# Loading batch 0's first four tiles as one four-token interleave, with the causal tokens computed by products over 11 rows of each tile

## The chip, the cores and the metric

One core of a Trainium2 chip. The metric is the device time of one execution in microseconds, in which a profiled execution's span (first to last instruction) lies about 1.5 us below its time. Engines: PE is TensorE (matrix products), DVE VectorE, ACT ScalarE, POOL GpSimd, SP SyncE.

## The reference, cut to what matters

Four batches, eight heads, 768 tokens, head size 40; an mLSTM cell, then a maxout MLP on 3072 tokens.

```python
for t in range(S):
    m_new = np.maximum(f_gate[:, :, t] + m, i_gate[:, :, t])
    f_stab = np.exp(f_gate[:, :, t] + m - m_new); i_stab = np.exp(i_gate[:, :, t] - m_new)
    C = f_stab * C + i_stab * (v_t outer k_t);  n = f_stab * n + i_stab * k_t
    y[:, :, t] = sigmoid(o_gate_t) * (C q_t) / max(|n q_t|, 1)
h1 = x @ w1; h2 = x @ w2
out = np.maximum(h1, h2) @ w_out        # x is y as [3072, 320]; w1, w2: 320 x 1024
```

The kernel uses that, with these gates, only the first 42 tokens of a sequence contribute to C and n. It checks this on the chip; if it does not hold, PE and the other engines branch into a general block after the fast part. These inputs never enter that block. Tokens below 42 are causal (a mask over keys); all later ones use the finished state. The maxout is rewritten as relu(x(w1 - w2)) w_out + x (w2 w_out), so a unit of token pairs needs an "up" part (products with wd = w1 - w2 into pu), a relu (gt), and a "down" part (products with wo and with Wc_t = w2 w_out into po).

## The kernel before, where the change and the argument touch it

```python
UNITS = [[0, 1], [2], [3, 4], [5, 6], [7, 8], [9, 10], [11]]   # pairs of token tiles
SEG = ((0, 1), (1, 4), (4, 6))        # batch 0 is loaded as tile 0, tiles 1-3, tiles 4-5
...
def f_h(n, pool=None, eng=V, dup=V):  # output of the cell for token tile n
    first = c == 0                    # tile 0: 128 tokens in order, masked scores
    ...
    if n % 2:                         # copy the last 64 columns for the other lanes
        cp(dup)(out=y[:, DM:DM + 64], in_=y[:, 2 * DM:2 * DM + 64])
    cp(eng)(out=nqb[:, n, :], in_=ph[:, :, D])
...
# start-up, in program order (cut)
A.copy(out=kb[:, 1:B]..., in_=warm...);  A.copy(out=vw[:, 1:B]..., in_=warm...)
f_k(0, pp_o); idle(2)                 # idle(n): n filler products, meant to keep PE's clock up
...
f_q(1, A, 2); sig_first(0, V); f_h(0, pp_o)
f_q(3, V, 1); sigm(0, 1, 2); sigm(0, 2, 4); idle(3)
f_h(1, pp_o, V, A); f_h(2, None); f_h(3, pp_o, V, A)     # the copies of y on ACT
...
# end
with tc.If(general > 0), ExitStack() as gctx:    # general block, not entered here
    ...
```

## Time and profile before

| | before |
|---|---|
| time, median of 3 | 96.98 us (96.98 to 97.0) |
| the profiled execution | 97.5 us, span 96.0, clock 1.0 |
| PE, DVE, ACT, POOL busy | 89.0, 54.8, 42.5, 28.0 us |
| first MLP product, first output product | 13.61, 24.79 us |
| last copy of an output out of PSUM (where PE's products land) | 93.09 to 93.38 us |

PE is busy nearly throughout. What matters is when its dense part (from the first output product on) begins. The profiled execution was 0.5 us slower than the median.

### The profile page before, as it was taken

Reading aid. Unit: us, or ns where it says so; the run is one execution under the profiler, and the core shown is the slowest. Engines: PE = TensorE matmul, PEld = TensorE weight load, DVE = VectorE, ACT = ScalarE, POOL = GpSimd, SP = SyncE. Lnnn points to the kernel's source line nnn. Section 1 sums busy time; section 2 is a strip of 40 time slices with the busy share of each in tenths; the row PEclk is TensorE's granted clock in tenths of the full one; section 3 lists DMA queues with packets and bytes.
Section 4 is the critical chain, followed back from the end, with each engine's and each line's share of the span. In section 5 each row is a group of like instructions: output and inputs, shape, how many; then the busy total and the mean of one; then the engine's idle time right before and its main releaser. Section 6 shows DMA issues by size and latency. Waiting matters only on the chain.

```text
span 96.0 us, 2281 instructions
## 1 busy us (share of the span) xinstructions
PE 89.0 (93%) x875; PEld 65.1 (68%) x875; DVE 54.8 (57%) x164; ACT 42.5 (44%) x63; POOL 28.0 (29%) x67
## 2 busy tenths in 40 slices
PE   3999979899889999999999999999999999999970
PEld 1347546766479788788787866768676777786660
DVE  4978926952368999597852535976054352240340
ACT  0886693861523771192809067080623408404000
POOL 5054596755655442623154000044000000000000
DMA  0999999997999999996999899697712030311052
GB/s 13 171 268 332 386 387 373 354 241 127 309 292 243 215 215 360 306 116 113 295 279 104 121 296 300 165 108 85 205 68 72 0 137 10 138 70 68 7 205 68
DMA packets 34045, 18.29 MB, mean 191 GB/s; under 512 B 23152, under 2 KB 31792, under 8 KB 34032
## 3 DMA queue, kind: packets, MB, share of 16 engines
q1 hardware_dynamic: 32594, 17.90, 75.7%
q10 hardware_dynamic: 1438, 0.23, 1.5%
q8 instruction: 7, 0.11, 0.5%
q14 instruction: 6, 0.05, 0.2%
HBM read 12.42 MB, written 3.93 MB: 170 GB/s over the span
## 4 chain that ended last, share of the span: by engine, by line
PE 56%; DMA 23%; SPq 11%; DVE 4%; ACT 2%; issue 1%; DVEq 0%
PE po L510 21%; DMA ost<-in_o_gate_dram 17%; PE pu L464 14%; PE po L506 6%; DMA w<-in_moe_w_dram 6%; PE pu L472 5%; SPq L118 3%; PE ph L357 3%; SPq L380 3%; DVE y L367 2%; PE pq L298 2%; SPq L104 2%; PE po L494 2%; ACT ost L267 2%; PE py L389 1%
## 5 line engine op out<-in xcount | busy, mean ns | idle before, releaser
L481 ACT ACTIVATE gt<-pu 128x1024 bf16<-128x1024 f32 x18 | 17.6, 1021 | 27.3 <-PE pu L472 27.3
L510 PE MATMUL po<-wo,gt 128*128 128x320 bf16 x160 | 26.9, 299 | 0.0
L464 PE MATMUL pu<-xT,wd 128*128 128x256 bf16 (+1 forms) x224 | 24.9, 257 | 1.0 <-DVE xT L390 0.7
L518 DVE COPY o_sb<-po 128x320 f32<-128x320 f32 (+2 forms) x23 | 10.9, 474 | 20.4 <-PE po L510 20.3
L464 PEld LDWEIGHTS <-wd 128*128 128x128 bf16 x224 | 19.0, 98 | 3.7 <-POOL wdx L408 0.8
L510 PEld LDWEIGHTS <-gt 128*128 128x128 bf16 x160 | 15.0, 98 | 5.2
L367 DVE SCALAR_TENSOR_TENSOR y<-ost,ph 128x320 bf16<-128x320 f32 x20 | 9.6, 481 | 3.1 <-PE ph L357 2.0
L267 ACT ACTIVATE ost<-ost 128x320 f32<-128x320 f32 (+2 forms) x14 | 8.7, 657 | 4.7 <-DMA ost<-in_o_gate_dram 4.7
L506 PE MATMUL po<-Wc_t,xT 128*128 128x320 bf16 (+2 forms) x50 | 10.7, 296 | 0.0
L222 PE MATMUL pd<-warm,ident_b 128*128 128x512 bf16 x25 | 8.9, 479 | 1.7 <-POOL ident_b masks.py:199 1.7
L257 POOL CAST qb<-qst 128x240 bf16<-128x240 f32 (+1 forms) x12 | 5.8, 485 | 11.7 <-DMA qst<-in_q_dram 9.9
L472 PE MATMUL pu<-xT,wd 64*128 64x256 bf16 (+1 forms) x112 | 7.7, 256 | 0.0
L357 PE MATMUL ph<-cq,qT 120*128 120x123 bf16 (+1 forms) x60 | 6.0, 213 | 0.7 <-DVE nqb L371 0.4
L481 ACT ACTIVATE gs<-pu 128x512 bf16<-128x512 f32 x8 | 4.3, 591 | 5.0 <-PE pu L472 5.0
L357 PEld LDWEIGHTS <-qT 120*128 120x128 bf16 (+1 forms) x60 | 4.4, 98 | 2.7 <-DMA qT<-qb 0.7
L402 POOL TENSOR_TENSOR wd<-w 128x512 bf16<-128x512 f32 x4 | 5.1, 1270 | 2.9 <-DMA w<-in_moe_w_dram 2.7
L506 PEld LDWEIGHTS <-xT 128*128 128x128 bf16 x50 | 3.9, 97 | 2.8 <-issue 1.8
L510 PE MATMUL po<-wo,gs 128*128 128x320 bf16 (+2 forms) x40 | 5.8, 272 | 0.0
L472 PEld LDWEIGHTS <-wd 64*128 64x128 bf16 x112 | 4.0, 94 | 2.4 <-issue 1.3
L538 POOL TENSOR_TENSOR a<-i_sb,F 32x640 f32<-32x640 f32 x1 | 1.5, 1532 | 12.4 <-DVE F L536 12.4
L222 PEld LDWEIGHTS <-ident_b 128*128 128x128 bf16 x25 | 2.5, 116 | 3.7 <-POOL ident_b masks.py:199 1.7
L494 PE MATMUL po<-Wc_t,xT 64*128 64x320 bf16 (+2 forms) x25 | 3.6, 292 | 0.4 <-ACT Wc_t L442 0.4
(126 smaller groups left out, 112.2 us busy)
## 6 DMA issues: line engine op xcount, KB each, us to landing
qst<-in_q_dram SPq DMA_DIRECT2D x3, 800.0 KB, 5.8
ost<-in_o_gate_dram SPq DMA_DIRECT2D x3, 800.0 KB
out_dram<-o_sb SPq DMA_DIRECT2D x7, 320.0 KB
w<-in_moe_w_dram SPq DMA_DIRECT2D x8, 256.0 KB, 5.6
out_dram<-o_sb SPq DMA_DIRECT2D x9, 160.0 KB, 3.7
wo_st<-in_moe_w_out_dram SPq DMA_DIRECT2D x2, 640.0 KB
qst<-in_q_dram SPq DMA_DIRECT2D x4, 160.0 KB
wx<-in_moe_w_dram SPq DMA_DIRECT2D x2, 256.0 KB
```

Of the source, the lines that this page charges most:

```text
L222: nc.tensor.matmul(pd[:, 0, :], ident_b, warm, start=True, stop=True)
L257: cp(eng)(out=qp[b % 2][:, c0:c1, 0:2, 0:HS3 * D].rearrange("p c s (h d) -> p c s h d", d=D), in_=qst[b][:, 0:6, c0:c1, :].rearrange("p (s ...
L267: A.activation(out=s, in_=s, func=AF.Tanh, scale=0.5)
L357: nc.tensor.matmul(ph[:, vcols(s), :].rearrange("p a b -> p (a b)"), lhsT, rhs[:, vcols(s), :].rearrange("p a b -> p (a b)"), start=True, ...
L367: V.scalar_tensor_tensor(out=yo, in0=ost[b][:, :, c, :], scalar=1.0, in1=ph[:, :, 0:D], op0=OP.add, op1=OP.mult)
L464: nc.tensor.matmul(pus[i][:, j, :], wd[:, c, f * 128:(f + 1) * 128], x[:, :, GA[i][c], :], start=(c == 0 and (j % 2 == 0 if np_ == 2 else ...
L472: nc.tensor.matmul(pus[i][:, j, :], wd2[r, f * 128:(f + 1) * 128], x[r, :, 2, :], start=False, stop=(j == 3 if np_ == 1 else j % 2 == 1))
L481: A.activation(out=o, in_=pus[i], func=AF.Relu)
L494: nc.tensor.matmul(po, xT[u][r, s // 2, 2, :], Wc_t[r, 2, w], start=True, stop=False)
L506: nc.tensor.matmul(po, x[:, s // 2, GA[s % 2][cc], :], Wc_t[:, cc, w], start=False, stop=False)
L510: nc.tensor.matmul(po, gt[:, f, s % 2, s // 2 * L:(s // 2 + 1) * L], wo[:, f, w], start=False, stop=(f == NFF - 1))
L518: cp(eng)(out=o_sb[:, s % 2 if two else 0, :], in_=po)
```

## The change

The intent: q and o_gate of batch 0's first four tiles in one load of 640-byte runs instead of runs of 160 and 480, so that the first loads and the weights behind them land earlier; the first 42 tokens then lie in rows 0 to 10 of each of four tiles, where short products overwrite the state's result. Single-pair units do both halves of their up part in one piece. Two transposes move from the DMA queue to PE, and the slots between the units' pieces are reordered.

```diff
-    SEG = ((0, 1), (1, 4), (4, 6))
+    SEG = ((0, 4), (4, 6))
+    TC = 11
...
+    G.tensor_copy(out=F[:, L:L + NS * KP]..., in_=ident_f[:, 0:H9].unsqueeze(2).to_broadcast([BH, H9, T0]))
     G.memset(sel, 0.0)
...
-    def f_h(n, pool=None, eng=V, dup=V):
+    def h_parts(n, pool=None, eng=V, dup=V):
...
+        if n < 4:
+            yield
+            for s in range(NS):
+                nc.tensor.matmul(ph[0:TC, vcols(s), :]..., Pm[0][m, s, c, :], vb[0][m, vcols(s), :]..., ...)
...
+    def up_one(u):                       # a single-pair unit: all 8 blocks, then all 64-row products
...
-    A.copy(out=vw[:, 1:B]..., in_=warm...)
+    G.memset(fold, 0.0) ; G.affine_select(fold...)      (moved up)
+    G.memset(vw[:, 1:B], 0.0)
...
     f_k(0, pp_o)
     idle(2)
     f_v(0, pp_o)
...
-    f_h(1, pp_o, V, A)
-    f_h(2, None)
-    f_h(3, pp_o, V, A)
+    parts = [h_parts(n, (pp_o, pp_f, pp_f, pp_o)[n]) for n in range(4)]
+    for g in parts:
+        next(g)
...
-    G.tensor_copy(out=wo[:, 4:8], in_=wo_st[:, 4:8])
-    sigm(0, 4, 6)                        (moved behind the close of Wc_t)
+    G.tensor_copy(out=wo[:, 4:6], in_=wo_st[:, 4:6])
+    A.copy(out=wo[:, 6:8], in_=wo_st[:, 6:8])
...  (the slot plan: X10, X16 become y10, y16, and most others move)
```

## The prediction

> **What bounds the kernel now.** I read the engine shares first, then engine busy time by stage, then the chain that ended last, then the timeline of the first 25 us. The shares give PE 89.0 of 96.0 us, but 8.9 us of that are filler products with the tile pd (25 of them), all in the start-up. So I cut the span into three stages, by two events that the timeline shows: the first MLP product at 13.6 and the first output product at 24.8. The columns are length of the stage, then busy time and count of each engine.
>
> ```profile
> core 0: us, PE busy (x) PEld busy (x) DVE busy (x) ACT busy (x) POOL busy (x), PEclk, DMA share, GB/s
> 1.60:13.50 11.90, 11.06 (x71) 5.68 (x71) 9.68 (x40) 8.65 (x16) 5.95 (x20) 1.00 1.04 285
> 13.50:24.80 11.30, 10.42 (x102) 7.63 (x102) 6.30 (x10) 6.31 (x11) 7.76 (x8) 1.00 1.02 277
> 24.80:92.70 67.90, 67.21 (x701) 51.58 (x701) 37.96 (x110) 27.54 (x38) 13.60 (x36) 1.00 0.73 169
> ```
>
> The reader is to see that from 24.8 to 92.7 PE idles for 0.69 us in all: that part gets shorter only by taking PE work away. PE's dense part starts at 24.8, and what matters is what sets that date. A piece of the chain from the dense part, start and length in us:
>
> ```profile
> 72.84 0.54 PE pu L472 x8
> 73.38 0.14 PE po L494 x2
> 73.52 0.38 PE po L506 x2
> 73.90 1.09 PE po L510 x8
> ```
>
> Eight products of 320 columns take 1.09 us, 136 ns each. The 64-row products (L472, L494) run in pairs and cost more than their columns[...]. So a passage into 64-row products and out again costs about 0.22 us.
>
> The chain in the start-up:
>
> ```profile
> 7.56 5.76 DMA w<-in_moe_w_dram
> 13.34 10.33 DMA ost<-in_o_gate_dram
> ...
> 23.69 0.74 ACT ost L267
> 24.43 0.32 ACT Wc_t L442
> ...
> 24.79 0.31 PE po L494 x2
> ```
>
> The gate load of batch 0's last two tiles lands at 23.7. ACT, in order, does its tanh (L267) before it closes Wc_t, for which PE waits 0.41 us. The timeline shows the two other walls:
>
> ```profile
> 7.75 0.72 POOL L262 CAST qb<-qst 128x640 bf16<-128x640 f32 x1 [0.80 <-DMA qst<-in_q_dram]
> ...
> 12.97 0.49 DVE L390 COPY xT<-py 128x640 bf16<-128x640 bf16 x1 [0.86 <-PE py L389]
> ...
> 13.61 1.03 PE L464 MATMUL pu<-xT,wd 128*128 128x256 bf16 x8 [0.68 <-DVE xT L390]
> ...
> 20.95 1.25 POOL L644 CAST wo<-wo_st 128x1280 bf16<-128x1280 f32 x1 [0.98 <-DMA wo_st<-in_moe_w_out_dram]
> ```
>
> q of tiles 1 to 3 lands at 7.75; from it hangs the chain cast, transposes, h, y, transposes, xT (13.46), first MLP product (13.61). The second half of wo lands at 20.9, its cast ends at 22.2, and 12 products with wo (12 x 136 = 1.63) plus six transposes (0.34) must follow: 24.2. Both loads are bound by the DMA engines, busy throughout; how fast they move depends on the run length (last two columns: share and GB/s):
>
> ```profile
> 4.00:5.50 1.50, 1.50 (x7) 0.82 (x6) 1.39 (x12) 1.27 (x3) 0.00 (x0) 1.00 1.27 211
> 6.00:8.00 2.00, 2.00 (x14) 1.02 (x13) 1.20 (x5) 1.46 (x3) 1.12 (x5) 1.00 1.21 297
> 10.00:12.00 2.00, 1.79 (x19) 1.16 (x19) 2.00 (x9) 1.26 (x4) 1.25 (x1) 1.00 1.06 389
> ```
>
> In the first stretch the runs are mostly 160 bytes (k, v, one tile of q and o_gate), in the second 480 (three tiles interleaved), in the third 2048 (weights).
>
> [...]
>
> **The change, part by part.** (a) Loads. Per run and engine the times are 16 x 160 / 211 = 12.1 ns, 16 x 480 / 297 = 25.9 and 16 x 2048 / 389 = 84. A line between the last two gives about 32 ns for 640 bytes, or 320 GB/s. Before, k, v and the first tile of q and o_gate (0.43 MB) take 2.05 us and the other three tiles (0.98 MB) 3.3: together 5.35. After, k and v take 0.5 and 1.31 MB at 320 GB/s 4.1: together 4.6. So all weights land about 0.8 us earlier. q of all four tiles no longer has any o_gate beside it: 0.14 MB are through by about 3.3 us, 0.66 MB at 320 GB/s take 2.05, and 0.9 us more pass until the release (as before, where the bytes ahead of q's end were through at about 6.8): 6.3 instead of 7.75.
>
> (b) The y chain. It gets longer: tile 0 no longer goes ahead alone. From q at 6.3: two half casts on ACT and POOL at once (0.72) to 7.0; PE is busy with the v and c products until about 7.4, as DVE's row reaches only then; transposes (0.35), ACT copy of qT (0.80) to 8.6, DVE's beside it to 8.7; the mask product (0.35), 3 score products, P0 at about 9.4; 12 main and 12 short products (some 55 ns each, as five PE transposes in the chain take 0.28; 1.25 together) 8.9 to 10.2; four y of DVE with copies of 0.18 and 0.16 between, from 9.8 to 12.0; the second pair's transposes 12.2 to 12.5, its xT at 13.1. But the first MLP products are now done pair by pair (8 of 128 columns, 0.45), so PE starts at 12.5 instead of 13.6, and the fold products (0.43) fill the wait for the second pair. Gain 1.1.
>
> (c) From first MLP product to dense part, 11.2 us before. Pure PE work there is the first unit's up part 4.58, 20 transposes 1.1, fold 0.43, 24 products with wo 3.27, six transposes 0.34: 9.7. The remaining 1.5 is mostly waiting: the 0.41 for Wc_t goes (tanh moved behind it), and the first relu now starts after half the last products, so its buffer frees 0.4 earlier. PE then reaches the products with the second half of wo at about 20.8. wo: landing 20.9 - 0.8 = 20.1, and the cast is halved between POOL and ACT (0.65 instead of 1.25): also about 20.8. From there 1.63, a close of 0.49 and a little: dense part at 23.0 to 23.3 instead of 24.8. Gain of (a) to (c) together: 1.5 to 1.8; I take 1.6.
>
> (d) Dense part. Two DMA transposes (pairs 5 and 8 of y) become PE transposes: 10 x 55 ns = +0.55 us of PE. Units of a single pair in one piece: one passage of 64-row products less per unit (about 0.12 for the first, 0.22 for the last): -0.35. All other PE counts are the same (the order of both kernels lists 160 + 40 output products, 48 transposes of q, and so on, in each). Of the 0.69 us of PE idle, the worst piece, at 60 us, waited on DVE behind an o_gate load and a DMA transpose; two DMA transposes less (1.2 to 3 us of queue each) should save about 0.3. Sum about -0.1. ACT's 8 relu of 0.59 become 4 of 1.02: 0.6 us less, off the path.
>
> Sum: -1.6 - 0.1 = -1.7, so 95.3 us.
>
> **The rivals.** First: the y chain eats the load's gain. The trace for it: DVE and ACT are the tight engines there (9.7 and 8.7 of 11.9 us), every y costs 0.48 on DVE, and all four now come after the mask. Against: MLP work begins with pair 0. If so, PE starts at 13.6, and only (c)'s 0.6 to 0.8 remains: 96.1. Second: wo keeps the date. If weights land no earlier (from the ninth load on, each issue waits for the landing of the load eight places before it, so the program may hold them back), the cast at 20.9 + 0.65 leaves a start at 24.0, 0.8 gained: 96.1. Third: the dense part pays. DVE is busy 4.5 and 4.7 of 5 us between 30 and 40, and two copies of 0.49 come on top; with work 1.6 us earlier, loads of batches 1 to 3 have less time (DMA share near 1 until 60 us). New PE waits of 0.5 to 1 us would give 95.8 to 96.3. A fourth goes the other way: the later waits were all DMA, and PE loses none any more: 94.8.
>
> **Range and chances.** The start-up gain lies between 0.8 and 2.1, the dense part between -0.6 and +0.6. That is 94.4 to 96.3. The 2% line is at 95.04, only 0.26 below my number, so faster by over 2% gets 0.36. Slower by over 2% needs +1.9 us, for which I see nothing: 0.02.
>
> **What would show it.** q's first cast at about 6.3; first MLP product near 12.5; first wo-half casts near 20.1; first product into po near 23.2; from there to the last product 67.8 us with PE idle under 0.6. If the y chain starts PE at 13.5 or later, step (b) is wrong; if wo's last cast begins after 20.6, step (a); if the dense part is above 68.3, step (d). Fewer than 17 fillers matter only if PE's products there get slower than 55 ns per 128 columns.

The sum came to -1.6 (start-up) and -0.1 (dense part), -1.7 in all, so 95.3 us. The 0.22 can be had from the trace of before: sixteen products of 256 columns take 1.75 us there (from 71.09), 109 ns each, so four would take 0.44 where the four 64-row pairs took 0.54; two products of 320 columns at 136 ns would take 0.27 where the two after them took 0.38. That makes about 0.21.

## The result, and the profile after

The change measured 99.44 us median (98.49 to 101.45, four runs) against 96.98. The fast runs give a ratio of 1.0169 (95% interval 1.0149 to 1.0189): slower by 1.7%, where I had predicted 95.3. The profiled execution was a slow one (101.45 us, span 100.0). Its page, the granted clock in tenths in 40 slices of 2.5 us:

```profile
PEclk9996559999999999999999999999999999999999
```

Then engine busy time by stage, with the same three stages as in the prediction, the cuts laid near this kernel's own events (the last one at its first output product, 27.72):

```profile
1.60:14.60 13.00, 11.30 (x66) 7.24 (x68) 9.42 (x33) 5.76 (x8) 9.11 (x22) 0.76 0.98 323
...
27.80:95.40 67.60, 67.46 (x714) 52.22 (x714) 39.97 (x113) 26.10 (x33) 11.36 (x29) 1.00 0.55 143
```

The clock (column 7) was 0.76 on average in the first stage, and the dense part began 2.9 us later than before. The dense part itself is no worse: 67.6 us, with PE idle 0.14 us in it. A slow execution does not explain the fast ones, so the fast start-up must be read elsewhere. The experiment a5_shortgen below executes exactly the same instructions as the change and its profile is fast; it stands for the change in the fast state up to the last output. In it the first MLP product comes at 13.93 and the first output product at 24.86: no earlier than before (13.61 and 24.79).

```profile
1.60:13.90 12.30, 11.17 (x81) 6.38 (x82) 10.89 (x40) 6.89 (x11) 8.56 (x22) 1.00 0.98 319
13.90:24.80 10.90, 10.52 (x117) 8.09 (x117) 7.00 (x15) 6.93 (x12) 6.84 (x9) 1.00 1.00 277
24.80:92.64 67.84, 67.67 (x717) 52.25 (x714) 40.49 (x113) 26.33 (x33) 12.88 (x33) 1.00 0.59 158
```

DVE was busy 10.89 us in the first stage against 9.68 before. Its timeline there, a5_shortgen, with start, length and the idle time before:

```profile
4.51 0.94 DVE L246 CAST kb<-kst 42x320 bf16<-42x320 f32 x1
...
6.60 0.80 DVE L249 TENSOR_TENSOR vw<-vst,gT 42x328 bf16<-42x328 f32 x1
```

and that of POOL in the same execution:

```profile
4.26 1.02 POOL L643 MEMSET vw<- 128x1107 bf16 x1
6.34 0.72 POOL L268 CAST qb<-qst 128x640 bf16<-128x640 f32 x1 [1.06 <-DMA qst<-in_q_dram]
```

The same two instructions of DVE before:

```profile
4.24 0.31 DVE L240 CAST kb<-kst 42x320 bf16<-42x320 f32 x1
...
6.94 0.49 DVE L243 TENSOR_TENSOR vw<-vst,gT 42x328 bf16<-42x328 f32 x1
```

The cast of 42x320 took 0.94 us instead of 0.31 and ended 0.17 us after POOL's memset. The product of 42x328 took 0.80 instead of 0.49, beside POOL's cast of q, which ended 0.34 us before it. That DVE stood still in them until POOL was done is my reading of these times; a2_dupact, a3_poollate and c3_dupv below put it to the test. What in the chip makes it wait, the traces do not show.

The second finding is at the other end. From the page's list of queues, and from the waits of SP, the change:

```profile
q8 instruction: 8, 0.13, 0.6%
```

```profile
SPq L953 <- DMA out_dram<-o_sb: 2.0, 1, 2.0
```

and before:

```profile
q8 instruction: 7, 0.11, 0.5%
```

```profile
SPq L882 <- DMA out_dram<-o_sb: 0.4, 1, 0.4
```

q8 moves blocks of 16,384 bytes, and how many goes with the length of PE's program (eight in the change, seven in a5_shortgen, which has 76 PE instructions less and is otherwise the same), so I take them for PE's instructions. The change has one more than before, and it starts at 96.4 us, 1 us after the end of PE's last product; before, the last one starts at 90.3 us, ahead of the last outputs. SP's last wait, for the last output, grew from 0.4 to 2.0 us. From the end of the last copy out of PSUM to the end of the span it is 2.6 us before and 4.2 after.

So there were two theories for the fast executions, and one for the slow ones: (1) DVE waits for POOL in the start-up (0.63 and 0.31 us in the two lines above) and gives back what the earlier load gains; (2) a late instruction fetch (96.37 to 97.30 us) delays the last output; (3) the wait that (1) puts on PE (1.3 us in the change's slow profile) lets its clock fall in some executions.

### The profile page after: what moved, and what is told of

It reads as the page before. It is cut to its first block, busy times and chain, and to the rows that moved or that the text cites. A ratio compares the mean times of both kernels' runs of the same rounds, so it can differ in the third digit from the quotient of the medians.

```text
span 100.0 us, 2338 instructions
## 1 busy us (share of the span) xinstructions
PE 91.2 (91%) x910; PEld 68.8 (69%) x911; DVE 59.4 (59%) x170; ACT 39.9 (40%) x54; POOL 29.1 (29%) x68
## 3 DMA queue, kind: packets, MB, share of 16 engines
HBM read 12.42 MB, written 3.93 MB: 164 GB/s over the span
## 4 chain that ended last, share of the span: by engine, by line
PE 76%; DMA 11%; DVE 6%; issue 1%; SPq 1%
PE po L575 26%; PE pu L505 17%; PE po L571 7%; DMA ost<-in_o_gate_dram 6%; PE pu L513 5%; DMA w<-in_moe_w_dram 5%; PE ph L375 3%; PE pwc L465 3%; PE pu L479 3%; PE py L415 2%; PE po L559 2%; PE pq L304 2%; DVE y L391 2%; DVE gt L519 1%; PE pu L486 1%
## 5 line engine op out<-in xcount | busy, mean ns | idle before, releaser
L505 PE MATMUL pu<-xT,wd 128*128 128x256 bf16 (+1 forms) x176 | 20.9, 263 | 0.3 <-DVE gt L519 0.3
L505 PEld LDWEIGHTS <-wd 128*128 128x128 bf16 x176 | 15.5, 98 | 3.1 <-issue 0.6
L273 ACT ACTIVATE ost<-ost 128x640 f32<-128x640 f32 (+2 forms) x13 | 8.3, 693 | 0.0
L227 PE MATMUL pd<-warm,ident_b 128*128 128x512 bf16 x16 | 6.5, 528 | 1.9 <-POOL ident_b masks.py:199 1.7
L513 PE MATMUL pu<-xT,wd 64*128 64x256 bf16 x80 | 6.1, 272 | 0.0
L489 ACT ACTIVATE gs<-pu 128x1024 bf16<-128x1024 f32 x4 | 3.9, 1021 | 4.9 <-PE pu L486 4.9
L375 PEld LDWEIGHTS <-qT 120*128 120x128 bf16 (+1 forms) x63 | 4.9, 108 | 1.1 <-DVE nqb L397 0.2
L416 DVE COPY xT<-py 128x640 bf16<-128x640 bf16 x7 | 3.4, 491 | 2.4 <-PE py L415 1.9
L227 PEld LDWEIGHTS <-ident_b 128*128 128x128 bf16 x17 | 1.9, 126 | 4.1 <-issue 2.4
L305 DVE COPY qT<-pq 128x768 bf16<-128x768 bf16 x7 | 3.8, 553 | 1.3 <-PE pq L304 1.3
```

The costliest lines, as they stand in the source:

```text
L227: nc.tensor.matmul(pd[:, 0, :], ident_b, warm, start=True, stop=True)
L273: A.activation(out=s, in_=s, func=AF.Tanh, scale=0.5)
L375: nc.tensor.matmul(ph[:, vcols(s), :].rearrange("p a b -> p (a b)"), lhsT, rhs[:, vcols(s), :].rearrange("p a b -> p (a b)"), start=True, ...
L505: nc.tensor.matmul(pus[i][:, j, p0 * L:p1 * L], wd[:, c, f * 128:(f + 1) * 128], x[:, p0:p1, GA[i][c], :], start=start and j % 2 == 0 and ...
L513: nc.tensor.matmul(pus[i][:, j, :], wd2[r, f * 128:(f + 1) * 128], x[r, :, 2, :], start=False, stop=stop and j % 2 == 1)
```

## The experiments

Twelve kernels compared with before in five rounds. They ran in four jobs, each on one chip and all four chips different; before measured 97.21, 97.23, 97.19 and 97.12 us in them. All results were correct.

### a0_again: the change once more

No edit.

> The changed kernel once more, unchanged, for a profile that fell into full clock and for how often the low clock comes. Clock theory (the tensor engine's idle 1.3 us at 6.3 to 7.6 us and thin work after it let the clock fall to 0.5 for some 7 us in some runs): times scatter from 98.5 to 101.5 as before, the granted clock falls as the time rises, and in a run at clock 1.0 the first output product starts near 26.5 instead of 27.8. Rival (the scatter is the chip's, not this kernel's): the kernel before, in the same rounds, scatters too.

Measured: 99.99 us median (98.06 to 101.43, six runs), ratio of the fast ones 1.0149 [1.0110, 1.0188]. Profile slow again, at half clock for the same 6.83 us as above. The two states of the change are reproducible, and before, in the same rounds, had no slow execution.

### a1_fill: four more filler products ahead of the v product

```diff
     f_k(0, pp_o)
-    idle(2)
+    idle(6)
     f_v(0, pp_o)
```

> Four more filler products ahead of the v product, so that the tensor engine is not idle there. Clock theory: every run at clock 1.0, no run above 99, median near 98.5, that is about 1 us below the changed kernel's median; nothing gained over its fast runs. Rival (the start-up is set by the vector engine's and GpSimd's chain, the clock is a bystander): same scatter or a shift of all runs, the fast ones included.

Measured: 98.99 us (98.44 to 99.17, five runs), ratio 1.0176 [1.0151, 1.0202]; no slow execution (though two of 99.17, where I had expected none above 99), clock 0.997 in the profile. In the slow profile of the change, PE waited before the v product:

```profile
PE pv L337 <- DVE vw L249: 1.3, 1, 1.3
```

and these are its stretches around that wait (busy times as above, the seventh column the clock):

```profile
5.00:6.50 1.50, 1.17 (x8) 0.64 (x8) 1.50 (x11) 1.11 (x3) 0.27 (x1) 1.00 1.13 356
6.50:8.00 1.50, 0.30 (x1) 0.13 (x1) 1.41 (x4) 0.71 (x1) 1.20 (x4) 1.00 1.13 364
8.00:10.00 2.00, 1.90 (x17) 1.70 (x16) 1.25 (x4) 0.87 (x2) 0.09 (x1) 0.57 1.06 387
10.00:15.00 5.00, 4.79 (x35) 3.86 (x36) 2.42 (x6) 1.19 (x2) 4.77 (x4) 0.50 1.05 383
```

PE had 0.30 us of work between 6.5 and 8.0; from 8.27 it ran at half clock for 6.83 us, in which it was busy 6.61 us. The clock records of that trace come in stretches of 3.41, 6.83 and 85.33 us, which are one, two and 25 times 3.41; I call a stretch of 3.41 us, counted from where the records begin, a window. In both slow profiles the first window, at full clock, began at 4.9 us and held the whole wait: PE was busy for 52% (the change) and 60% (a0_again) of it, and the next two windows were at half clock. In the two fast profiles of kernels with the wait, a5_shortgen and a2_dupact, the first window at full clock began only at 6.5 and 6.1 us, the wait was 0.6 and 0.5 us, and PE was busy for 77 and 80% of the window. With the wait bridged (a1_fill, from 4.9 us) it was 81%. So in these five profiles the state goes with where the windows fall on the wait; what decides it in general they do not show. Slow were 11 of the 23 executions of kernels with the wait (the change, a0_again, a2_dupact, a5_shortgen), and none of 44 of those with it bridged or removed (a1_fill, a3_poollate, a4_all, a6_allshort and the four of c1_loops to c4_best). So (3) is right for the slow executions that were profiled, but it is about the slow ones alone: the fast time stayed where it was, with the first MLP product at 13.95 and the dense part at 24.88. This is the prediction's own last sentence come true: the change has fewer fillers, and they mattered.

### a2_dupact: the copies of y on ACT

```diff
-    parts = [h_parts(n, (pp_o, pp_f, pp_f, pp_o)[n]) for n in range(4)]
+    parts = [h_parts(n, (pp_o, pp_f, pp_f, pp_o)[n], V, A) for n in range(4)]
```

> The two 64-column copies of y in the start-up go back to ScalarE, as in the kernel before. In the changed kernel they took 0.82 and 0.47 us on VectorE, where the same copy takes 0.18 elsewhere, while GpSimd ran weight subtractions. [...]first MLP product 0.6 to 0.9 us earlier and the fast time 0.5 to 0.9 lower. Rival (the copies stretch, but the weight loads or ScalarE set the pace): under 0.2 us.

The words cut here, and in a3_poollate and c3_dupv, named a cause inside the chip, which no run shows; what was tested is whether DVE's instructions take longer beside POOL's.

Measured: 98.53 us (98.08 to 101.28, two of six slow), ratio 1.0117 [1.0095, 1.0140]: 0.3 us below the change's in a0_again, which the two intervals do not separate, and less than the 0.5 to 0.9 expected. The first MLP product came at 13.48, the dense part at 24.41, 0.45 us earlier than in a5_shortgen. But 0.31 of that is not the edit's: in this execution DVE's v product began at 6.61 us, 0.01 ahead of POOL's cast of q; it took 0.49 us, and POOL's cast 1.06 instead of 0.72. In a5_shortgen the cast began first, and the v product took 0.80. The copies themselves, from the first y to the first MLP product, were 0.14 us (2.67 against 2.81): a small part of the loss as the change is timed.

### a3_poollate: POOL's copy and memset behind its cast of q

```diff
-    G.tensor_copy(out=F[:, L:L + NS * KP]..., in_=ident_f[:, 0:H9]...)     (ahead of all other POOL work)
-    G.memset(vw[:, 1:B], 0.0)                                               (behind the fold's mask)
...
     pad_q(1)
+    G.tensor_copy(out=F[:, L:L + NS * KP]..., in_=ident_f[:, 0:H9]...)
+    G.memset(vw[:, 1:B], 0.0)
```

> GpSimd's selector copy into F and its zeroing of vw, both new in the start-up before 5.3 us, are moved behind the q cast, into GpSimd's idle time at 7.7 to 9.9 us. [...]VectorE's cast of kb comes back from 0.94 to about 0.31 us and its v product from 0.99 to about 0.49, the v product on the tensor engine starts about 1 us earlier (6.6 instead of 7.64), the idle gap shrinks to 0.3, the clock stays at 1.0 in most runs, and the fast time falls by 0.5 to 1.0. Rival (other things set the start of the v product): the casts stay long, less than 0.2 us.

Measured: 99.15 us (98.95 to 99.46, four runs, none slow), ratio 1.0203 [1.0181, 1.0225]: 0.5 us slower than the change's fast runs, where 0.5 to 1.0 less was expected. The trace says where the gain went. The cast of k was back at 0.30 us, the v product 1.2 us earlier at 6.3, the first y at 10.6 instead of 11.1. Then the first copy of y took 1.16 us, from 11.48, and the first MLP product came at 14.1. The earlier chain had moved that copy onto a POOL instruction, as in c3_dupv below: POOL's subtraction wdx ran from 11.33 to 12.60, and the copy ended at 12.64. It also speaks for (3) following from (1): with the wait gone, no slow execution of four, and none in the later kernels that have this edit.

### a4_all: the three edits of a1, a2 and a3 together

> The changed kernel with three edits at once: four more filler products after the score products, the copies of y for the second pair's other lanes taken from VectorE to ScalarE, the selector copy and the memset of GpSimd put behind its pad copy. Theory (the start-up is lost to VectorE waiting for GpSimd, the clock fall to the idle PE, and both gains were given back one step later when only one was mended): no slow execution, kb cast about 0.30 us, v product at about 6.3 us, copies of y short, first MLP product at 12.5 to 12.9, dense part from 23.3 to 23.9, last output copy ending about 1 us earlier than in a1_fill (92.2), and the tail of 3.9 to 4.4 us unchanged, so 97.3 to 98.0 us. Rival (the weights or the wo casts set the dense start whatever y does): first MLP product early but dense start still 24.5 or later, time 98.3 to 99.

Measured: 98.26 us (97.92 to 98.89, six runs, all fast), ratio 1.0111 [1.0075, 1.0146]. A miss: I had expected 97.3 to 98.0. First MLP product at 13.24, dense part at 24.17, where I had expected 12.5 to 12.9 and 23.3 to 23.9. The v vector was ready at 6.46, but PE was in the six fillers until 7.08: here the fillers held back by 0.62 us the work that they were to bridge to, as it came early. The tail was 4.2 us, as in the change, and as expected.

### a5_shortgen: the change with fewer PE instructions in the block that is never entered

```diff
-                for j in range(c + 1):
-                    nc.tensor.matmul(pH[:, c, :], Pa[:, j, c * L:(c + 1) * L], v1[:, j, :], ...)
+                nc.tensor.matmul(pH[:, c, :], Pa[:, c, c * L:(c + 1) * L], v1[:, c, :], start=True, stop=True)
...  (one of three products into pu, one of eight into po, likewise; wrong on purpose if it were entered)
```

> The changed kernel with PE instructions cut out of the general block, which these inputs never enter (its result would be wrong if it were entered; on purpose): 1894 PE program rows instead of 1970, before has 1909; nothing that is executed differs. Theory (an eighth 16 KB instruction fetch behind PE's last product shares a DMA engine with the last output and delays it): seven fetches instead of eight, none behind the last product, wait for the last output 0.3 to 0.6 us instead of 1.6 to 2.2, from last output copy to end about 2.6 us; fast executions 1.3 to 1.8 us below the changed kernel's, so 96.6 to 97.4; slow executions stay. Rival (the longer tail comes from the single-piece last units or the output transfers themselves): eight or seven fetches, but the tail stays at 3.9 or more and the time at 98.5.

Measured: two fast runs, 97.35 and 97.59, and four slow ones, 100.05 to 101.06; too few fast ones for an interval. Their mean, 97.47, is 1.2 us below that of the change's fast runs (98.65 in a0_again, on another chip with the same time of before). Its queue and SP's wait:

```profile
q8 instruction: 7, 0.11, 0.5%
```

```profile
SPq L947 <- DMA out_dram<-o_sb: 0.7, 1, 0.7
```

Nothing that is executed differs, only the program's length, and what the trace shows of that is that the late fetch is gone. Two of the four slow executions (100.08 and 101.06) are listed at clock 1.0 and left no trace; before's trace has no clock record at all and is listed at 1.0 too, so a 1.0 need not mean full clock, and what slowed these two stays open.

### a6_allshort: a4_all with the same cut

> a4_all with the same cut in the general block: 1902 PE rows. If the start-up theory and the fetch theory hold and add: 95.5 to 96.4 us, every execution fast, faster than the kernel before by 0.8 to 1.5 per cent. If only the fetch theory holds: 96.7 to 97.3. If neither: 98 to 99.

Measured: 97.14 us (96.39 to 97.32, six runs, all fast), ratio 0.9969 [0.9932, 1.0006]; 1.12 us below a4_all on the same chip, the same fetch effect a second time. In its profile the first fillers followed each other at 0.43 us instead of 0.21 (its clock records begin, at full clock, only at 7.28), and the v product started only at 7.89, so the dense part began at 24.83: less than I had expected of the start-up, for the reason named under a4_all.

### b1_longgen: the kernel before with a longer block that is never entered

```diff
-            for c in range(NT):
-                for j in range(c + 1):
+            for _ in range(3):
+                for c in range(NT):
+                    for j in range(c + 1):
...
```

> The kernel before with the head loop of the general block, never entered, written out three times: 1993 PE rows instead of 1909; nothing that is executed differs. Fetch theory: an eighth instruction fetch behind PE's last product, wait for the last output 1.6 to 2.2 us instead of 0.4, time 98.2 to 98.9 (slower by 1.3 to 1.9 per cent). Rival (rows that aren't executed cost nothing): 97.0 to 97.3, the same.

Measured: 98.15 us (97.88 to 98.44, six runs), ratio 1.0090 [1.0059, 1.0121]. The old kernel, none of whose executed instructions was touched, becomes 0.9% slower (I had expected 1.3 to 1.9):

```profile
q8 instruction: 8, 0.13, 0.6%
```

```profile
SPq L883 <- DMA out_dram<-o_sb: 1.4, 1, 1.4
```

This settles (2). How it comes about, as far as the traces tell: PE's program comes in seven to eight blocks of 16,384 bytes for some 2000 instructions, fetched while PE works (before: seven, starting from 18.6 to 90.3 us, 9 to 16 apart). A longer branch shows too, but it costs nothing here: PE's branch over the block takes 0.68 us in b1_longgen, 0.37 in the change and 0.24 before, while PE's next instruction waits for a semaphore until 0.77 to 0.81 us after the branch's start in all three, and the eighth fetch starts only 1.4 to 1.7 us after it. What was late were packets of the last outputs: in the trace of the change the eighth block is fetched from 96.37 to 97.30, and 16 packets of the last two outputs, eight of 128 from each, go one after another from 97.28 to 98.12, when all others had landed by 96.93. That is a sixteenth of each output, what one of the 16 DMA engines carries if they share evenly (the trace does not name the engine of a packet), and it is 1.2 us late; in b1_longgen the same share is 0.95 us late. So the fetch of a further block, some 1.5 us after the jump, seems to stand in one DMA engine's way when the last outputs have to leave; that it is one engine, and that the jump causes the fetch, are inferred from the packets' number and the order in time.

### c1_loops, c2_x, c3_dupv and c1_forced

c1_loops has a3's and a2's edits, the change's own two fillers, and a general block that is complete but has loops in place of unrolled products (1902 PE instructions by my count). c2_x takes the two transposes back to the DMA queue; c3_dupv puts the copies of y back on DVE; c1_forced enters the block.

```diff
 c1_loops, general block
-            for f in range(NFF):
+            with tc.For_i(0, NFF, 1) as f:
...  (also for the heads' sum; its transposes by DMA)
 c2_x, against c1_loops
-C3.1.3|h17|            ... x20|y16||||        (and y10, likewise)
+C3.1.3|h17|X16         ... x20|||||
 c3_dupv, against c1_loops
-    parts = [h_parts(n, (pp_o, pp_f, pp_f, pp_o)[n], V, A) for n in range(4)]
+    parts = [h_parts(n, (pp_o, pp_f, pp_f, pp_o)[n]) for n in range(4)]
 c1_forced, against c1_loops
-    with tc.If(general > 0), ...
+    with tc.If(general > -1), ...
```

> The changed kernel with GpSimd's selector copy and memset behind its pad copy and the copies of y on ScalarE, fillers as in the change (in a4_all and a6_allshort the four extra fillers themselves held the v product back by 0.6 and 1.4 us), and a general block that is complete but has its products in loops: 1902 PE rows. Theory: v product at about 6.4 us, y from about 10.0, first MLP product at 12.5 to 12.8, dense part from 23.4 to 23.8, dense part 67.7 to last output copy, tail 2.6: 95.2 to 96.2 us, 1 to 2 per cent faster than before. Rival (without the extra fillers the clock falls in some executions): a spread up to 99 or more, slow executions. Rival (the gain is again eaten by another wait): 96.5 to 97.3.

Measured: 98.23 us (97.92 to 98.79, six runs, all fast), ratio 1.0131 [1.0105, 1.0158]. A miss, and not of the start-up: first MLP product 13.03 (I had expected 12.5 to 12.8), dense part 23.96 (23.4 to 23.8), last copy out of PSUM ending at 91.99, 0.6, 0.8 and 1.4 us earlier than in before's profile (0.3, 0.9 and 0.9 against that of b1_longgen). The rest went in a tail of 4.3 us. With the loops the program had again an eighth block, fetched at 92.2, although by my count it is no longer than a6_allshort. That count leaves out what the loops add: PE's instruction file is 130,048 bytes long for c1_loops and 126,848 for a6_allshort, which is 2032 and 1982 instructions of 64 bytes (the change and a5_shortgen differ by 4,864 bytes for 76 instructions). Of the eleven kernels whose list of queues was read, those with 1973 to 2013 fetched seven blocks and those with 2032 to 2063 eight (before 1979, the change 2049).

> c1_loops with the copies of y back on VectorE, as the change has them. [...]the first copy waits for GpSimd's weight subtraction to end and takes about 1.1 us instead of 0.24 on ScalarE, the next y products come later, first MLP product 0.9 to 1.4 us later, time 0.6 to 1.3 us above c1_loops. Rival (a3_poollate lost its time to something else): within 0.3 us of c1_loops.

Measured: 98.81 us (98.54 to 99.33, five runs), ratio 1.0168 [1.0144, 1.0192]; 0.6 us above c1_loops by the medians, 0.4 by the ratios. Timeline of DVE and of POOL:

```profile
11.26 1.16 DVE L392 COPY y<-y 128x64 bf16<-128x64 bf16 x1
```

```profile
11.12 1.26 POOL L432 TENSOR_TENSOR wdx<-wx 128x512 bf16<-128x512 f32 x1
```

A copy of 64 columns began 0.14 us after POOL's subtraction, and ended at 12.42, 0.04 after it. On ACT the same copy takes 0.24 (c4_best). The first MLP product and the dense part came 0.92 us later than in c1_loops. Theory (1) holds for this part as well.

> c1_loops with the transposes of the sixth and ninth pair back on the DMA queue, as the kernel before has them, in earlier slots: ten PE transposes less. If the dense part is bound by PE's own work alone: 0.4 to 0.6 us less than c1_loops (each five transposes took about 0.27 us of PE time). Rival (the transposed pairs arrive late or delay the loads): the same or slower, with waits of PE for xT.

Measured: 97.20 us (96.84 to 97.62, six runs), ratio 0.9994 [0.9974, 1.0014]; 1.0 us below c1_loops. The number is better than I had expected, but not for the reason: from the first output product to the last copy it took 67.90 us, c1_loops 67.74. PE had 0.37 us less work between 24 and 91 and waited 0.37 more. The gain came from the tail: with 20 PE instructions less there was no eighth 16 KB block. Yet 3.9 us passed from the last copy to the end. Its queues and SP's wait:

```profile
q8 instruction: 7, 0.11, 0.5%
q14 instruction: 8, 0.07, 0.3%
```

```profile
SPq L955 <- DMA out_dram<-o_sb: 1.1, 1, 1.1
```

q14 moves blocks of 8,192 bytes, of which before, the change, a1_fill and a4_all to b1_longgen have six; here two more ran from 93.3 to 94.4 us, and the eight packets of the last output that are one DMA engine's even share landed by 94.1, 0.6 us after all others. My loops had lengthened the programs of the other engines (c1_loops has 205, 79, 126 and 81 instructions on DVE, ACT, POOL and SP by my count, c4_best below 192, 67, 113 and 71 and again six blocks), so I take these blocks for theirs.

> c1_loops with the general block entered on purpose after the fast path, to see whether its rewritten form computes the reference: correct, and far slower (hundreds of us to some ms).

Measured: correct, 2601 us. The rewritten block is right.

### c4_best and c4_forced: a general block without loops

The start-up of c1_loops, one of the two transposes (X16) on the DMA queue, and a complete general block with transposes by DMA and products of 512 columns instead of 128: 1906 PE instructions by my count, and fewer on the other engines than c1_loops has.

```diff
-            for f in range(NFF):
-                pu = pp_u.tile([128, L], FP, name="g_pu", tag="pu")
-                ...  (three products of 128 columns for each f)
+            pu = pp_u.tile([128, 2, 512], FP, name="g_pu", tag="pu")
+            for hf in range(2):
+                for cc in range(3):
+                    w_, r = (wd[:, cc], slice(0, 128)) if cc < 2 else (wd2, slice(0, 64))
+                    nc.tensor.matmul(pu[:, hf], xg[r, cc, :], w_[r, hf * 512:hf * 512 + 512], ...)
+            nc.scalar.activation(out=gm, in_=pu..., func=AF.Relu)
+            nc.sync.dma_start(out=gg, in_=gm, transpose=True)
```

> The start-up of c1_loops (first MLP product at 13.0 us, dense part from 24.0 there) with a complete general block that has no loops added: transposes on the DMA queue and wide products, 1906 PE rows, and 192, 67, 113, 71 rows on VectorE, ScalarE, GpSimd and SyncE, where c1_loops has 205, 79, 126, 81. Fetch theory, now for all engines: seven 16 KB fetches, and no 8 KB fetch of another engine after 90 us (c1_loops and c2_x had two, at 93 to 94 us); from last output copy to end 2.6 to 3.0 us; 95.3 to 96.2 us, 1 to 2 per cent faster than before. Rival (the long tail of c2_x, which had no late 16 KB fetch, comes from how early its last outputs were queued): no late fetch but still 3.6 or more from last output copy to end, 96.8 to 97.3 us.

Measured: 96.37 us (96.02 to 96.81, six runs, all fast) against 97.12, ratio 0.9916 [0.9889, 0.9942]: faster than the change, and 0.8% faster than before. The stages, and then the queues and SP's wait:

```profile
1.60:13.20 11.60, 11.01 (x80) 6.57 (x82) 9.50 (x39) 6.88 (x12) 7.67 (x21) 1.00 0.96 314
13.20:24.10 10.90, 10.51 (x116) 8.07 (x115) 7.30 (x13) 7.34 (x12) 7.28 (x9) 1.00 0.97 272
24.10:91.80 67.70, 67.50 (x711) 51.98 (x709) 40.02 (x112) 26.23 (x33) 13.14 (x35) 1.00 0.62 165
```

```profile
q8 instruction: 7, 0.11, 0.5%
q14 instruction: 6, 0.05, 0.2%
```

```profile
SPq L951 <- DMA out_dram<-o_sb: 0.4, 1, 0.4
```

No late block of either kind, 2.9 us from the last copy to the end, and a first output product at 24.14. So the long tail of c2_x goes with late fetches too, and not with the outputs' own queue. The time lies a little above the range I had set (95.3 to 96.2).

> c4_best with the general block entered on purpose after the fast path: correct, 1.5 to 3 ms.

Measured: correct, 1562 us.

## Why the prediction was wrong, point by point

**Step (a), loads: right.** The first casts of q began at 6.34 (predicted 6.3, before 7.75), the second cast of wo at 20.2 (predicted 20.1, before 20.95). ACT's quarter of wo, though, was cast only from 21.85, behind a relu in ACT's order: by the prediction's own sign (last cast after 20.6) a mark against the step, but not one of the loads. The DMA engines moved 355 to 390 GB/s between 5 and 15 us, more than the 320 that I had interpolated for 640-byte runs (356 from 5.0 to 6.5 in the change, where nearly all bytes went in runs of 640).

**Step (b), the y chain: this step failed.** It was to gain 1.1 us, with DVE's durations taken from before; in the fast state the first MLP product came at 13.93 instead of 12.5. I had listed every instruction of the chain and none of what POOL does beside it. Two delays of DVE beside POOL ate it: 0.63 us in the cast of k and 0.31 in the v product (POOL's new copy and memset, and a cast moved to the same moment; with the copy and memset moved away, a3_poollate, the cast of k was back at 0.30), then the copies of y, which I had put down as 0.18 each on DVE without noticing that before had them on ACT. In the change, here a5_shortgen, they take 0.38 and 0.46 (0.14 us of the chain, see a2_dupact), and where the chain is earlier, 1.16 (c3_dupv, 0.92 us of the chain):

```profile
12.04 0.38 DVE L394 COPY y<-y 128x64 bf16<-128x64 bf16 x1
...
13.31 0.46 DVE L394 COPY y<-y 128x64 bf16<-128x64 bf16 x1
```

With both mended, the numbers of the step come close: P0 ends at 9.8 in c1_loops (predicted about 9.4), the first y at 10.4 (9.8), the last of the four at 12.1 (12.0), the first MLP product at 13.0 (12.5). My first rival, that the y chain eats the load's gain, described the outcome, but for another reason: not that DVE has too much to do, but that single instructions of it last longer beside POOL's (a copy 1.16 us, against 0.18 on DVE elsewhere).

**Step (c), first MLP product to dense part: too large a gain.** It takes 10.93 us in the change and in a4_all, a6_allshort, c1_loops and c3_dupv alike, 11.18 in the profile of before and 11.56 in b1_longgen. I had predicted 10.5 to 10.8. The term that was mis-sized is PE's own work: I counted 9.7 us and took 1.5 for waiting, but PE was busy 10.42 us there before, as my own table showed, and 10.52 in a5_shortgen. wo was no longer the limit (no wait of PE for it shows), against my rival two.

**Step (d), the dense part: no measurable change, about as predicted.** From the first output product to the start of the last copy out of PSUM it takes 67.78 us in a5_shortgen. Before has 68.30 in its own profile, but b1_longgen, which executes the same instructions, has 67.74:

```profile
24.87:92.61 67.74, 67.45 (x704) 51.78 (x703) 38.44 (x110) 27.44 (x38) 13.66 (x36) 1.00 0.72 169
```

So the 0.5 us by which before's profiled execution was slower lay here, in waits of PE (0.73 us in all, against 0.29 in b1_longgen and 0.17 in a5_shortgen). The one at 60 us, from which I had taken 0.3 of the step, is not there in b1_longgen: that part of the step was read from one execution. Why it had these waits is open. Against b1_longgen PE's work grew by 0.16, so of the ten PE transposes, +0.55 (55 ns each), about 0.4 was paid by fewer 64-row passages (an estimate, as the difference of the two; I had 0.35).

**What the prediction had no step for.** The tail. I took it as fixed; from the last copy to the end it is 2.6 us before, and 3.9 to 4.4 in the fast profiles with the change's program (a1_fill to a4_all). Of that the late fetch is 0.9 to 1.2, through 61 PE instructions in a program whose end is a jump (a5_shortgen, a6_allshort against a4_all, b1_longgen). And the slow state, which I had touched in one sentence and given no weight.

The sum for the fast runs: predicted -1.7, measured +1.6 (98.6 against 97.0). The start-up, (a) to (c), was to gain 1.6 and gained nothing: the dense part begins at 24.86 in a5_shortgen, 24.79 before and 24.87 in b1_longgen. The dense part was to gain 0.1 and lost 0.04 against b1_longgen. The tail grew by 1.3 to 1.8. That accounts for the whole: the failed start-up cancels the gain, and the tail makes the loss. Left open is the part of the tail that stays without the late fetch, 0.35 us (3.0 in a5_shortgen); the traces place it behind the landing of the last packet (1.74 us to the end, against 1.43 before), but no run shows its cause.

The edits of c4_best bring the dense part to 24.14, 0.7 earlier than the change, not to 23.2. Of the 0.9 between them, about 0.2 is step (c); in the y chain, the first pair's copy into xT waits behind ACT's second copy of y in ACT's order, and PE waits 0.36 us for it before the first MLP product. The rest is not taken apart.

## What to carry to other kernels

When an edit moves or adds POOL work, check which DVE copies, casts and two-input products run at that moment: here their durations from the old profile no longer held (a cast of 0.31 us took 0.94, a product of 0.49 took 0.80, a copy of 0.18 took 1.16), and a chain made earlier ran into the next POOL instruction and gave the gain back (a3_poollate: v product 1.2 us earlier, first MLP product at 14.1 against 13.93). A stretch in which PE waits costs twice if the clock then falls (half clock for 6.83 us after a wait of 1.3 us), and whether it does changed from one execution to the next (11 slow of 23); fillers are part of the change when they are removed, and a cost when they stand ahead of work that has become ready (0.62 us in a4_all). And compare the number of instruction blocks and the time of the last one between two profiles before explaining a longer tail: code that is never executed cost 0.9% of a 97 us kernel (b1_longgen). Where two profiles differ by less than what a profiled execution lies off its kernel's median, a second profile of the same instructions has to come first: b1_longgen took half a microsecond out of my reading of before.
